# Windowed attention and a gated layer: one GpSimd select for identity and mask, and a new order of the opening table

## The chip, the core and the metric

The kernel runs on one core of a Trainium2 chip. A core has five engines with a queue of instructions each: TensorE (PE, matrix products; PEld is its loading of weights), VectorE (DVE), ScalarE (ACT), GpSimd (POOL) and SyncE (SP). Each works through its own queue in order and waits on semaphores for the others. Data moves between memory (HBM), the on-chip SBUF and the accumulators (PSUM, eight banks of 128 x 512 floats) by 16 DMA engines; loads are issued here by POOL, stores and transposes by SP. The metric is the device time of one execution in microseconds (us), as the median of several runs. Beside it stands one execution that was profiled; its span is the time from its first to its last instruction.

## The reference

Eight sequences of 576 positions, eight heads of 64. Each position attends to itself and the 63 before it; the result of all heads, 512 wide, is one token of a gated layer with 1536 hidden units.

```python
scores = (q @ k.T) / 8                      # per batch and head, 576 x 576
mask   = (rel >= 0) & (rel < 64)            # rel = query position - key position
attn   = softmax(where(mask, scores, -1e9)) # per row
x      = (attn @ v), heads side by side     # 4608 tokens x 512
g      = x @ w_gate                         # 512 -> 1536
out    = (g * sigmoid(g) * (x @ w_val)) @ w_out   # 1536 -> 512
```

## The kernel before

**Tiling.** The 4608 tokens are 36 *chunks* n of 128 and 9 *groups* c of 512 (four chunks each). Work on a chunk goes through these methods, each of which records operations on engines:

- `load_qk(n)`, `load_v(n)`: POOL issues the loads of q, k and v, with a cast to bf16 (two and one; twice as many where a chunk crosses two sequences). Buffers are rings: 6 for q and k (`NQ`), 10 for v (`NV`).
- `T`, `TE`: PE transposes q or k into a PSUM bank; ACT or DVE copies that to `qT`, `kT`. From chunk 8 on `TD` does it instead: SP issues two DMA transposes, k then q. Chunks 0 and 1 come over SP's and ACT's own queues (`first_loads`), as float, are cast by `first_cast`, transposed by `first_T` and copied by `first_ev`.
- `S(n)`: PE makes the scores in two banks, ACT takes the exponentials (line 790) into `pt`; for chunks 0 to 3 the mask is added before by a product with the identity (`bias`, line 759), for the others `M(n)` lets DVE multiply by a 0/1 mask (line 795).
- `A0`, `A1`: PE multiplies with v in two halves; a column of ones beside v (written once per buffer by `init_va`) gives the sum. `R(n, half)`: DVE's reciprocal and product (lines 875 and 878).
- `X`, `XE`: PE transposes the result, ACT or DVE copies it to `xT`. `XD` does it by a DMA transpose.

Work on a group:

- `FM(c, f, t0, t1)`: PE makes gate and value of hidden block f (of 12) for tokens t0 to t1 (line 977); `Ft`: ACT's tanh (line 996); `Fu`: DVE's two products into `uu` and `hT` (lines 1005 and 1007).
- `OM(c, u)`: twelve products with `Wo` (line 1017) make 128 rows of output; `OE`: ACT or DVE copies them, SP stores them.

Weights come in pieces by `load_w` and `load_wo`, on POOL's queue among the loads.

**Order.** The recorded operations are played on each engine in the order of recording. `_Graph.plan` finds the waits: an operation waits for the last one that wrote what it reads, or that read or wrote what it writes, unless an earlier wait of its engine covers it. Between two operations of the same engine it waits only where the second reads what the first wrote (not on PE).

The opening is a table written out by hand, `OPENING`: some 300 entries of a method, its arguments and the PSUM banks it is given. It covers the attention of chunks 0 to 11, all gated blocks of groups 0 and 1, the outputs of group 0, the scores of chunk 12 and all loads up to chunk 17. After it, `build` runs groups 2 to 8 in loops: `F` blocks, the outputs of the group before, and between them `block(n)` for the attention of chunks 12 to 19, then `pair(n)` for two chunks at a time from 20 on. `block(19)` makes chunk 20's scores on its way. At one place in group 3, the loop makes one chunk's scores alone before the pairs begin.

**What sets up the opening.** `init` (line 606) lets DVE fill the zero operand `wz` of the warm-up products, zero `ident` and `nmask`, and write the ones into all ten v buffers. POOL then makes the identity by one select over 128 x 128 (`init_pool_a`, line 625) and the additive mask by four selects over 64 x 64 (`init_mask`, line 633), and DVE the 0/1 mask from it. POOL's loads come after these five selects.

The head of the old table:

```python
    ("first_cast", ("q", 1, "act"), ()),
    ("load_qk", (2,), ()),
    ("load_v", (0,), ()),
    ("warm", (11,), (0,)),
    ("bias", (0,), (5, 3)),
```

Of the kernel before, what the change touches and what calls it, by code (L numbers as in the profile page):

```python
# [5 lines left out]
ALU = mybir.AluOpType  # L6

B, H, S, D = 8, 8, 576, 64
DM, DFF = H * D, 1536
T = B * S  # L10
# [20 lines left out]
class _Graph:  # L31
# [30 lines left out]
    def plan(self):  # L62
# [6 lines left out]
        for o in self.ops:  # L69
# [78 lines left out]
class _Program:  # L148
# [46 lines left out]
OPENING = [  # L195
    ("first_cast", ("q", 1, "act"), ()),
    ("load_qk", (2,), ()),
    ("load_v", (0,), ()),
    ("warm", (11,), (0,)),
    ("bias", (0,), (5, 3)),  # L200
    ("first_cast", ("k", None, "dve"), ()),
    ("first_T", ("k",), (6,)),
    ("first_cast", ("q", 0, "dve"), ()),
    ("first_T", ("q",), (1,)),
    ("first_ev", ("q", 0, "act"), ()),
    ("bias", (1,), (2, 4)),
    ("first_ev", ("k", 1, "dve"), ()),
    ("first_ev", ("q", 1, "act"), ()),
    ("T", ("q", 2), (7,)),
    ("load_v", (1,), ()),  # L210
    ("load_qk", (3,), ()),
    ("first_ev", ("k", 0, "dve"), ()),
    ("S", (0,), ()),
    ("T", ("k", 2), (0,)),
    ("TE", ("k", 2, "dve"), ()),
    ("load_v", (2,), ()),
    ("load_v", (3,), ()),
    ("S", (1,), ()),
    ("load_w", ("v", 0, 1), ()),
    ("bias", (2,), (1, 6)),  # L220
    ("A0", (0,), (3, 0)),
    ("load_w", ("g", 0, 1), ()),
    ("TE", ("q", 2, "dve"), ()),
    ("S", (2,), ()),
    ("load_w", ("g", 2, 4), ()),
    ("A1", (0,), ()),
    ("R", (0, 0), ()),
    ("A0", (1,), (4, 5)),
    ("A1", (1,), ()),
    ("R", (1, 1), ()),  # L230
    ("load_w", ("v", 2, 4), ()),
    ("T", ("q", 3), (7,)),
    ("T", ("k", 3), (1,)),
    ("warm", (2,), (6,)),
    ("TE", ("q", 3, "dve"), ()),
    ("bias", (3,), (5, 6)),
    ("load_qk", (4,), ()),
    ("load_w", ("v", 1, 2), ()),
    ("TE", ("k", 3, "act"), ()),
    ("S", (3,), ()),  # L240
    ("R", (1, 0), ()),
    ("A0", (2,), (7, 3)),
    ("A1", (2,), ()),
    ("R", (0, 1), ()),
    ("R", (2, 0), ()),
    ("X", (1,), (0,)),
    ("XE", (1, "act"), ()),
    ("A0", (3,), (2, 1)),
    ("R", (2, 1), ()),
    ("load_w", ("g", 1, 2), ()),  # L250
    ("A1", (3,), ()),
    ("X", (0,), (3,)),
    ("X", (2,), (5,)),
    ("XE", (2, "act"), ()),
    ("FM", (0, 0, 128, 256, 2), (4, 6)),
    ("load_w", ("g", 4, 6), ()),
    ("load_w", ("v", 4, 6), ()),
    ("R", (3, 1), ()),
    ("R", (3, 0), ()),
    ("X", (3,), (0,)),  # L260
    ("XE", (3, "act"), ()),
    ("XE", (0, "dve"), ()),
    ("FM", (0, 0, 0, 128, 2), (1, 7)),
    ("Ft", (0, 0, 0), ()),
    ("load_qk", (5,), ()),
    ("FM", (0, 0, 256, 512, 2), (3, 2)),
    ("load_v", (4,), ()),
    ("FM", (0, 2, 0, 256, 2), (0, 5)),
    ("Fu", (0, 0, 0), ()),
    ("Ft", (0, 0, 256), ()),  # L270
    ("Ft", (0, 0, 128), ()),
    ("Ft", (0, 2, 0), ()),
    ("FM", (0, 3, 0, 256, 2), (1, 7)),
    ("Fu", (0, 0, 128), ()),
    ("Ft", (0, 3, 0), ()),
    ("Fu", (0, 0, 256), ()),
    ("FM", (0, 3, 256, 512, 2), (4, 2)),
    ("T", ("q", 4), (6,)),
    ("load_qk", (6,), ()),
    ("Fu", (0, 3, 0), ()),  # L280
    ("Ft", (0, 3, 256), ()),
    ("FM", (0, 2, 256, 512, 2), (1, 3)),
    ("Fu", (0, 3, 256), ()),
    ("Ft", (0, 2, 256), ()),
    ("Fu", (0, 2, 0), ()),
    ("TE", ("q", 4, "act"), ()),
    ("FM", (0, 1, 128, 256, 2), (2, 7)),
    ("Ft", (0, 1, 128), ()),
    ("Fu", (0, 2, 256), ()),
    ("load_w", ("g", 6, 8), ()),  # L290
    ("FM", (0, 1, 0, 128, 2), (4, 0)),
    ("Ft", (0, 1, 0), ()),
# [1024 lines left out]
```

## Time and profile before

| what | value |
|---|---|
| median of 3 runs | 335.31 us (334.59 to 336.04) |
| profiled execution: time | 333.98 us |
| profiled execution: span | 331.4 us |
| granted TensorE clock, mean | 1.00 |
| PE busy | 323.7 us, 98% of the span |
| DVE busy | 224.7 us, 68% |
| ACT busy | 128.3 us, 39% |
| POOL busy | 110.7 us, 33% |
| POOL's loads (q0 software_dynamic) | 117312 packets, 18.36 MB |

The profiled execution is 2.6 us longer than its span, and 1.3 us below the median. A busy time says how long an engine worked, not what it was waited for: PE's matrix products overlap each other, and their ends are modelled, so for PE the distance from one start to the next says more than the sum of durations. A row of a timeline gives the start, the time it took, engine, source line, operation, what it writes and reads, and in brackets how long the engine sat idle before and what ended that. A row on DMA issues gives how many were issued, their size, and the median time from issue to landing.

### The profile page before, as it was taken

How to read it: one execution, taken by the hardware profiler on the slowest of the kernel's cores; microseconds unless marked ns; L12 is line 12 of the kernel's file. 1: busy time of each engine (PE TensorE's matmuls, PEld its weight loads, DVE VectorE, ACT ScalarE, POOL GpSimd, SP SyncE). 2: the span in 40 equal slices, each digit the busy share in tenths (PEclk: the TensorE clock that was granted, in tenths of full speed). 3: DMA queues.
4: the chain of work that ended last, by engine and by line, in shares of the span. 5: the costliest groups of instructions: out<-in, count | busy, mean ns of one | idle time of the engine just before them, and what ended most of it. 6: DMA issues, size and time to landing. Idle time of an engine off the chain costs nothing.

```text
span 331.4 us, 8401 instructions
## 1 busy us (share of the span) xinstructions
PE 323.7 (98%) x3511; PEld 166.2 (50%) x3511; DVE 224.7 (68%) x490; ACT 128.3 (39%) x239; POOL 110.7 (33%) x141
## 2 busy tenths in 40 slices
PE   7799899999999999999999999999999999999996
PEld 3587475555444544445454545454545444444444
DVE  5578896967866866667777777767676776565520
ACT  2756644343333543434242433333424222232222
POOL 7999993194364453333435151000000000000000
PEclk9999999999999999999999999999999999999999
DMA  9999999999999999999999999715140202000012
GB/s 169 150 177 169 171 191 141 171 135 170 169 167 148 191 154 174 173 160 158 149 126 108 135 124 130 128 53 110 47 113 33 65 33 64 34 32 35 35 60 102
DMA packets 169515, 40.19 MB, mean 121 GB/s; under 512 B 155904, under 2 KB 164992, under 8 KB 169472
## 3 DMA queue, kind: packets, MB, share of 16 engines
q0 software_dynamic: 117312, 18.36, 82.8%
q1 hardware_dynamic: 50976, 20.66, 33.3%
q10 hardware_dynamic: 1184, 0.59, 0.7%
q8 instruction: 28, 0.46, 0.6%
q14 instruction: 15, 0.12, 0.1%
HBM read 37.75 MB, written 9.44 MB: 142 GB/s over the span
## 4 chain that ended last, share of the span: by engine, by line
PE 92%; DVE 2%; POOL 2%; DMA 1%; ACT 1%; issue 1%; POOLq 0%
PE ps L977 56%; PE ps L1017 27%; PE ps L780 3%; PE ps L832 2%; PE ps L905 2%; DMA kn<-in_k_dram 1%; PE ps L1049 1%; PE ps L947 1%; DVE uu L1005 1%; POOL va L710 1%; POOL qn L647 1%; DVE hT L1007 0%; PE ps L730 0%; ACT sig L996 0%; ACT qT L664 0%
## 5 line engine op out<-in xcount | busy, mean ns | idle before, releaser
L1005 DVE SCALAR_TENSOR_TENSOR uu<-sig,ps 128x512 bf16<-128x512 bf16 (+2 forms) x122 | 76.0, 623 | 57.5 <-ACT sig L996 57.5
L977 PE MATMUL ps<-xT,Wg 128*128 128x512 bf16 (+2 forms) x488 | 113.7, 355 | 0.3
L977 PE MATMUL ps<-xT,Wv 128*128 128x512 bf16 (+2 forms) x488 | 113.3, 355 | 0.0
L996 ACT ACTIVATE sig<-ps 128x512 bf16<-128x512 f32 (+2 forms) x122 | 66.7, 551 | 82.7 <-PE ps L977 82.4
L1017 PE MATMUL ps<-Wo,hT 128*128 128x512 bf16 x420 | 95.9, 379 | 0.0
L1007 DVE SCALAR_TENSOR_TENSOR hT<-uu,ps 128x512 bf16<-128x512 bf16 (+2 forms) x122 | 76.3, 626 | 4.2
L977 PEld LDWEIGHTS ps<-xT,Wv 128*128 128x128 bf16 x488 | 47.1, 98 | 46.5 <-DVE uu L1005 0.2
L977 PEld LDWEIGHTS ps<-xT,Wg 128*128 128x128 bf16 x488 | 44.6, 98 | 42.2 <-issue 0.4
L1017 PEld LDWEIGHTS ps<-Wo,hT 128*128 128x128 bf16 x420 | 40.9, 98 | 49.2
L647 POOL DMA_DIRECT2D qn<-in_q_dram x38 | 34.9, 932 | 68.2 <-DMA qT<-qn 60.8
L790 ACT ACTIVATE pt<-ps 128x512 bf16<-128x512 f32 x72 | 38.0, 600 | 41.3 <-PE ps L780 41.2
L710 POOL DMA_DIRECT2D va<-in_v_dram x40 | 35.4, 911 | 24.0 <-PE ps L905 19.4
L664 ACT ACTIVATE ost<-ps 128x512 f32<-128x512 f32 (+2 forms) x26 | 15.0, 577 | 64.1 <-PE ps L1017 63.1
L647 POOL DMA_DIRECT2D kn<-in_k_dram x38 | 34.9, 936 | 0.9 <-issue 0.7
L795 DVE TENSOR_TENSOR pt<-pt,mask 128x512 bf16<-128x512 bf16 x64 | 23.8, 419 | 1.2 <-ACT pt L790 1.0
L666 DVE COPY ost<-ps 128x512 f32<-128x512 f32 (+1 forms) x12 | 7.9, 657 | 23.7 <-PE ps L1017 11.9
L878 DVE TENSOR_TENSOR xb<-ps,rc 128x256 bf16<-128x256 f32 x40 | 17.0, 425 | 1.4
L780 PE MATMUL ps<-qT,kT 64*64 64x64 bf16 (+1 forms) x864 | 16.0, 203 | 0.7 <-DVE kT L666 0.3
L780 PEld LDWEIGHTS ps<-qT,kT 64*64 64x64 bf16 x864 | 12.5, 108 | 6.2 <-issue 3.0
L832 PE MATMUL ps<-va,pt 64*64 64x65 bf16 x600 | 12.4, 196 | 1.5 <-issue 1.0
L832 PEld LDWEIGHTS ps<-va,pt 64*64 64x64 bf16 x600 | 8.3, 106 | 8.7 <-issue 3.0
L875 DVE RECIPROCAL rc<-ps 128x4 f32<-128x4 f32 x40 | 7.0, 175 | 6.1 <-PE ps L832 6.1
(57 smaller groups left out, 103.1 us busy)
## 6 DMA issues: line engine op xcount, KB each, us to landing
out_dram<-ost SPq DMA_DIRECT2D x35, 256.0 KB, 3.1
va<-in_v_dram POOLq DMA_DIRECT2D x32, 128.0 KB, 16.8
qn<-in_q_dram POOLq DMA_DIRECT2D x30, 128.0 KB, 15.2
kn<-in_k_dram POOLq DMA_DIRECT2D x30, 128.0 KB, 15.4
Wo<-in_moe_w_out_dram POOLq DMA_DIRECT2D x2, 768.0 KB, 16.2
Wg<-in_moe_w_gate_dram POOLq DMA_DIRECT2D x5, 256.0 KB, 6.7
Wv<-in_moe_w_val_dram POOLq DMA_DIRECT2D x5, 256.0 KB, 7.3
fk<-in_k_dram SPq DMA_DIRECT2D x1, 512.0 KB, 4.9
```

What stands on the lines that cost most here:

```text
L647: self.g.op("pool", lambda e, d=d, a=a: e.dma_start(d, a), writes=ks, dma=True)
L710: g.op("pool", lambda e, d=d, a=a: e.dma_start(d, a), writes=ks, dma=True)
L780: r = e.matmul(sv[h][o:o + 64, c, q0:q1], self.kT[ps, c, kk:kk + 64], qT[ps, c, q0:q1], start=not biased, stop=not biased or c == 3 and kk ...
L790: g.op("act", lambda e, po=po, si=si: e.activation(po, si, ACTF.Exp, scale=SCALE), reads=[bk], writes=[pk])
L795: "dve", lambda e: e.tensor_tensor(po, po, m, ALU.mult), reads=[pk, "mask"], writes=[pk]))
L832: r = e.matmul(av[half][ws, j, :], pt[ks, h, ws], vv[ks, h, 0:65], start=key == q[0], stop=key == q[-1])
L878: g.op("dve", lambda e, xo=xo, rb=rb, a=av[half]: e.tensor_tensor(xo, a[:, :, 0:64], rb, ALU.mult), reads=[bk, ("rc", ir)], writes=[("xb", ...
L977: r = e.matmul(bank[:, 0:n], W[:, kk, f * 128:f * 128 + 128], xT[:, kk, t0:t1], start=(kk == 0), stop=(kk == NK - 1))
L996: self.g.op("act", lambda e: e.activation(sig[:, 0:n], G[:, 0:n], ACTF.Tanh, scale=0.5), reads=[gk], writes=[("sig", i)])
L1005: g.op("dve", lambda e: e.scalar_tensor_tensor(uu[:, 0:n], sig[:, 0:n], 1.0, G[:, 0:n], ALU.add, ALU.mult), reads=[("sig", i), gk], writes ...
L1007: g.op("dve", lambda e: e.scalar_tensor_tensor(hT[:, f, t0:t1], uu[:, 0:n], 0.5, V[:, 0:n], ALU.mult, ALU.mult), reads=[("uu", i), vk], wr ...
L1017: r = e.matmul(OB[:, :], hT[:, f, 128 * u:128 * u + 128], self.Wo[:, f, :], start=(f == 0), stop=(f == NF - 1))
```

## The change

Four things change.

1. **The selects.** DVE fills a tile `tri` of 128 x 130 with ones, and POOL makes one select over 128 x 129 of it: one where the column is beyond the row, zero elsewhere. DVE takes the difference of two shifted views as the identity, and makes the additive mask by four multiplications of 64 x 64 of it. The 0/1 mask comes later, as an entry of the table (`mask01`), and so do the ones in the v buffers.
2. **The table.** It has the same work in another order, with other banks. Chunk 3's q and k are loaded before chunk 2's. Four half blocks of the gated layer (`FM` of blocks 3, 0, 2 and 0) stand before X(2) and X(3); in the old table X(0), X(1) and X(2) stand before the first. The loads of chunks 11, v8, 10, v10 follow `load_wo(0, 6)`, then chunk 9; in the old table it was chunk 10, 8, `load_wo(0, 6)`, 9, 11, v8. SP's transposes come in the order of chunks 8, 10, 9, 11; before it was 10, 8, 9, 11. There are 13 warm-up products in place of 14. Some copies change their engine: q0 and q1 of the first chunks, X(1), X(4), q5 and q6 go to DVE; k0, k1, X(0), q2, k7, X(10) and two output copies go to ACT.
3. **Waits.** An operation of ACT or DVE that writes what one of the last two of its own engine read or wrote now waits for that one too.
4. **The scores made alone** in group 3 are chunk 21's; in the kernel before they are chunk 20's, which `block(19)` makes too, and chunk 21's are not made there: the first pair reads for it what chunk 17 left in that buffer. The number of instructions is the same.

```diff
             for d, kind in deps:
-                if kind != "sync" and d.eng == e and not d.dma and (e == "pe" or kind != "raw") and not o.dma and e != "pool":
+                near = e != "pe" and not d.dma and npos[e] + 1 - d.pos < 3
+                if kind != "sync" and d.eng == e and not d.dma and (e == "pe" or kind != "raw" and not near) and not o.dma and e != "pool":
                     continue
...
 OPENING = [
+    ("init_va", (8, 9), ()),
+    ("warm", (11,), (7,)),
+    ("tri_select", (), ()),
+    ("ident_sub", (), ()),
+    ("warm", (1,), (6,)),
     ("first_cast", ("q", 1, "act"), ()),
+    ("load_qk", (3,), ()),
     ("load_qk", (2,), ()),
+    ("mask_half", (0,), ()),
+    ("mask_half", (64,), ()),
+    ("bias", (0,), (7, 0)),
...
     ("first_T", ("q",), (1,)),
-    ("first_ev", ("q", 0, "act"), ()),
+    ("first_ev", ("q", 0, "dve"), ()),
+    ("init_va", (0, 1), ()),
...
+    ("TE", ("q", 3, "dve"), ()),
...
+    ("mask01", (), ()),
+    ("first_ev", ("q", 1, "dve"), ()),
+    ("S", (1,), ()),
+    ("A0", (0,), (5, 0)),
+    ("A1", (0,), ()),
+    ("R", (0, 1), ()),
+    ("init_va", (1, 2), ()),
...
+    ("S", (2,), ()),
+    ("TE", ("k", 3, "act"), ()),
+    ("A1", (1,), ()),
...
+    ("S", (3,), ()),
...
+    ("load_wo", (0, 6), ()),
...
+    ("load_qk", (11,), ()),
...
+    ("load_v", (8,), ()),
...
+    ("TD", (8,), ()),
...
+    ("load_qk", (10,), ()),
...
+    ("load_v", (10,), ()),
...
+    ("load_qk", (9,), ()),
...
+    ("TD", (10,), ()),
...
+    ("TD", (9,), ()),
...
+    ("TD", (11,), ()),
...
+    ("OM", (0, 2), (3,)),
...
+    ("A0", (8,), (1, 0)),
+    ("S", (9,), (2, 4)),
...
-        g.op("dve", lambda e: e.memset(ident[:, :], 0.0), writes=["ident"])
-        g.op("dve", lambda e: e.memset(self.nmask[:, :], 0.0), writes=["nmask"])
+        g.op("dve", lambda e: e.memset(self.tri[:, :], 1.0), writes=["tri"])
...
-        self.init_va(0, self.NV)
...
+    def tri_select(self):
+        tri = self.tri[:, 0:129]
         self.g.op("pool", lambda e: e.affine_select(
-            out=ident[:, :], in_=ident[:, :], compare_op=ALU.not_equal, fill=1.0, base=0,
-            pattern=[[-1, 128]], channel_multiplier=1), writes=["ident"])
-    def init_mask(self):
-        for p0, c0, op in ((0, 0, ALU.is_ge), (0, 64, ALU.is_gt), (64, 0, ALU.is_gt), (64, 64, ALU.is_ge)):
...
+            out=tri, in_=tri, compare_op=ALU.is_ge, fill=0.0, base=-1,
+            pattern=[[1, 129]], channel_multiplier=-1), writes=["tri"])
+    def ident_sub(self):
+        self.g.op("dve", lambda e: e.tensor_tensor(self.ident[:, :], self.tri[:, 1:129], self.tri[:, 0:128], ALU.subtract),
+                  reads=["tri"], writes=["ident"])
+    def mask_half(self, p):
+        t = self.tri[p:p + 64, 1 + p:65 + p]
+        own, past = self.nmask[p:p + 64, p:p + 64], self.nmask[p:p + 64, 64 - p:128 - p]
+        self.g.op("dve", lambda e: e.tensor_scalar(own, t, 30000.0, -30000.0, ALU.mult, ALU.add),
+                  reads=["tri"], writes=[("nmask", p, 0)])
+        self.g.op("dve", lambda e: e.tensor_scalar(past, t, -30000.0, None, ALU.mult),
+                  reads=["tri"], writes=[("nmask", p, 1)])
...
         self.first_loads()
         self.init()
-        self.init_pool_a()
-        self.init_mask()
...
                     if (c, u, s) == alone:
-                        self.S(pair_from)
-                        self.M(pair_from)
+                        self.S(pair_from + 1)
+                        self.M(pair_from + 1)
                         self.share()
```

More of the change, by code (lines that the diff above doesn't have):

```diff
@@ L236 @@
[L236 to L239, printed above, removed]
+    ("X", (0,), (5,)),
+    ("warm", (1,), (4,)),
     ("S", (3,), ()),
     ("R", (1, 0), ()),
-    ("A0", (2,), (7, 3)),
-    ("A1", (2,), ()),
-    ("R", (0, 1), ()),
-    ("R", (2, 0), ()),
[L246 to L252, printed above, removed]
@@ L507 @@
-    ("OE", (0, 1, "dve"), ()),
 ]
@@ L759, in bias @@
             self.g.op("pe", lambda e, bv=bv: e.matmul(bv, self.ident[:, :], nm, start=True, stop=False),
-                      reads=["nmask", "ident"], writes=[bk])
+                      reads=[("nmask", p, i) for p in (0, 64) for i in range(2)] + ["ident"], writes=[bk])
         self.held["bias", n] = bb
```

480 lines of the change are left out of this document (240 added, 240 removed), and 11 rows, old and new, of the table OPENING.

## The prediction

> **What bounds the kernel now.** I read the page's DMA slices and chain first, then the busy time by stretch, then TensorE's timeline where it is not full.
>
> ```profile
> DMA  9999999999999999999999999715140202000012
> PE 92%; DVE 2%; POOL 2%; DMA 1%; ACT 1%; issue 1%; POOLq 0%
> ```
>
> TensorE is 92% of the chain that ends last. The DMA engines are full for the first two thirds, so a load's place in POOL's queue is a time.
>
> ```profile
> 0.00:5.70 5.70, 4.50 (x11) 1.64 (x12) 2.31 (x17) 1.49 (x2) 3.72 (x12) 1.00 0.66 182
> 5.70:19.40 13.70, 11.01 (x292) 7.14 (x290) 8.75 (x24) 8.29 (x16) 13.70 (x19) 1.00 1.96 153
> 19.40:42.40 23.00, 21.82 (x377) 15.89 (x377) 19.44 (x53) 13.90 (x32) 23.00 (x29) 1.00 1.99 174
> 42.40:83.70 41.30, 41.30 (x484) 24.07 (x473) 32.12 (x78) 16.88 (x35) 22.69 (x28) 1.00 1.80 160
> ```
>
> The columns are the stretch in us, its length, then PE, PEld, DVE, ACT and POOL. The opening table's matmuls end at 83.7. PE idles 2.7 us between 5.7 and 19.4 (13.70 - 11.01), 1.2 us up to 42.4, and not at all from there to 83.7. An order of the opening can win only what lies before 42.4, and keeps it only if loads and transposes are ready earlier too.
>
> ```profile
> 8.81 0.45 PE L780 MATMUL ps<-qT,kT 64*64 64x128 bf16 x24
> 9.52 0.45 PE L780 MATMUL ps<-qT,kT 64*64 64x128 bf16 x24
> 13.81 0.41 PE L780 MATMUL ps<-qT,kT 64*64 64x128 bf16 x22
> 15.35 0.56 PE L832 MATMUL ps<-va,pt 64*64 64x65 bf16 x17 [0.97 <-issue]
> 17.67 0.39 PE L977 MATMUL ps<-xT,Wg 128*128 128x128 bf16 x4
> 26.39 0.45 PE L780 MATMUL ps<-qT,kT 64*64 64x128 bf16 x24 [0.22 <-DVE uu L1005]
> 35.81 0.40 PE L730 MATMUL ps<-ident,kn 128*128 128x128 bf16 x4 [0.34 <-DVE uu L1005]
> 37.20 0.45 PE L780 MATMUL ps<-qT,kT 64*64 64x128 bf16 x24 [0.34 <-DVE kT L666]
> 64.96 2.75 PE L1017 MATMUL ps<-Wo,hT 128*128 128x512 bf16 x12
> 67.64 0.45 PE L780 MATMUL ps<-qT,kT 64*64 64x128 bf16 x24
> 68.02 2.76 PE L1017 MATMUL ps<-Wo,hT 128*128 128x512 bf16 x12
> 70.85 0.65 PE L780 MATMUL ps<-qT,kT 64*64 64x128 bf16 x44
> ```
>
> These are, in order: scores of chunks 0, 1 and 3; a stop of 0.97 us that no wait explains; the first matmul of the gated layer; three of the later waits; an output of group 0, the scores of chunk 9, another output, and the scores of chunk 11 (with chunk 10's).
>
> **The change, part by part.** *One select.* POOL's five selects become one.
>
> ```profile
> 1.46 0.29 POOL L625 TENSOR_SCALAR_AFFINE_SELECT ident<-ident 128x128 bf16<-128x128 bf16 x1 [1.01 <-DVE wup L612]
> 1.71 1.36 POOL L633 TENSOR_SCALAR_AFFINE_SELECT nmask<-nmask 64x64 bf16<-64x64 bf16 x4
> 3.37 1.01 POOL L647 DMA_DIRECT2D qn<-in_q_dram  x1 [0.30 <-issue]
> 37.05 1.23 POOL L647 DMA_DIRECT2D qn<-in_q_dram  x1
> 39.65 1.24 POOL L647 DMA_DIRECT2D kn<-in_k_dram  x1
> qn<-in_q_dram POOLq DMA_DIRECT2D x2, 128.0 KB, 17.5
> kn<-in_k_dram POOLq DMA_DIRECT2D x2, 128.0 KB, 17.6
> 7.37 1.29 DVE L666 COPY kT<-ps 128x512 bf16<-128x512 bf16 x2
> 1.56 1.43 DVE L621 MEMSET va<- 128x128 bf16 x10
> 14.29 1.09 ACT L790 ACTIVATE pt<-ps 128x512 bf16<-128x512 f32 x2 [0.65 <-PE ps L780]
> ```
>
> The select ends at 1.46 + 0.29 = 1.75 instead of 1.71 + 1.36 = 3.07, so the first load leaves 1.32 us earlier, and with it the whole full queue: I carry a head start of 1.32. The subtraction and four half masks go to DVE, idle then; their first readers wait on the casts of k (after 5.7) anyway. Nothing on the path; without that idle time they would cost some five short DVE operations.
>
> *Up to the first gated layer.* Chunk 0's scores still wait for the first q transpose and a strided copy of 0.65 us (half of 1.29): 8.8, as now. On DVE the copy of q for chunk 1 now stands behind two va memsets (0.14 each, a tenth of 1.43), a copy of q3 and the 0/1 mask, so chunk 1's scores come at about 10.2 (now 9.52). Chunk 2's wait for k2's copy behind R(0,1) and a memset, about 12.6. Chunk 3's wait for k3's copy, on ACT behind chunk 2's two exponentials (1.09 from 13.1, then a copy of some 0.6): about 14.7 (now 13.81). X(1), its copy and the banks it holds then put A0(2) at 16.0, and the first gated matmul at 17.1 (now 17.67). But X(2), X(3) and k4's transpose come after three half blocks. Where both kernels have done the same work, near 26, I find them level: gain 0, between -0.5 and +1 (the unexplained 0.97 may go, since the attention is less dense there).
>
> *26 to 42.4.* Now PE loses 0.9 us in the three waits shown and about as much in smaller steps, 1.9 in all by the distances of starts. In the new order k and q of a chunk are copied a block of the gated layer before their scores. I still find waits: 0.25 for k6's copy, 0.38 for a bank held by Fu(0,10), 0.30 for XE(5). That leaves 1.2 gained at 42.4, with 0.2 from before 26.
>
> *42.4 to 57.* DVE works without a gap from 40.3 to 46.8 now.
>
> ```profile
> 40.32 0.68 DVE L1005 SCALAR_TENSOR_TENSOR uu<-sig,ps 128x512 bf16<-128x512 bf16 x1
> 47.00 0.69 DVE L1005 SCALAR_TENSOR_TENSOR uu<-sig,ps 128x512 bf16<-128x512 bf16 x1 [0.18 <-ACT sig L996]
> ```
>
> The new order adds five memsets there or before (0.7) and the copies of q5, q6 and X(4) that ACT did, and gives k7's to ACT. With FM(1,1) and FM(1,4) waiting for banks that Fu(0,6) and Fu(1,3) read, 0.4 goes back: gain 0.8. Two output copies moved to ACT cost nothing: ACT is busy 16.88 of 41.30 there.
>
> *Loads and transposes.* POOL's loads and SP's transposes move with the table.
>
> ```profile
> 55.86 1.19 SPq L748 DMA_TRANSPOSE kT<-kn  x1
> 57.10 1.39 SPq L751 DMA_TRANSPOSE qT<-qn  x1
> 60.03 1.27 SPq L751 DMA_TRANSPOSE qT<-qn  x1
> 69.67 1.27 SPq L751 DMA_TRANSPOSE qT<-qn  x1
> qT<-qn SPq DMA_TRANSPOSE x1, 7.3
> qT<-qn SPq DMA_TRANSPOSE x1, 9.1
> ```
>
> These are chunk 9's two, the last of chunk 11's and of chunk 12's; the landing times are those of the second and third row. Now chunk 9's q lands at 64.4 (57.10 + 7.3) for scores at 67.64, chunk 11's at 69.1 for 70.85: 1.7 us in hand. In the new order the loads of q11, k11, v8 and v10 stand ahead of chunk 9's. Four loads, 0.87 apart ((39.65 - 37.05) / 3) with equal time to landing, are 3.5; less the head start, 2.2 later: 66.6 and 71.3, for SP still issues chunk 11 after chunk 9. The scores of 9 would be asked for at 64.96 - 0.8 - 0.5 (chunk 8's A is now behind) + 2.68 + 0.25 = 66.6: just met. Those of 11 follow 0.38 + 0.25 + 2.7 + 0.1 later, at 70.0, and wait 1.3. Behind them in PE's queue stands all else. Bounds: no wait, if the loads keep their landing; 4 us more, if chunk 10's two transposes, now just ahead of chunk 9's, delay them at the present pace (four in 69.1 - 55.86 = 13.3, 3.3 each, less the 2.6 by which chunk 10 is loaded earlier). I take 1.3, the row nearest to it being chunk 11's own.
>
> *The rest.* Waits between near operations of ACT or DVE: most were ordered by an earlier wait; some 0.05 us beside PE. One warm-up matmul more stands ahead of the bias and two fewer later, all where PE waits for casts or copies. Making chunk 21's scores instead of chunk 20's is the same instructions; its transposes were issued blocks before. Nothing.
>
> **Sum.** 0.8 - 1.3 = -0.5: the span goes from 331.4 to 331.9, and the profiled execution from 333.98 to 334.5. The median of the runs shown, 335.31, lies 1.3 above that execution; with it I forecast 335.8.
>
> [...] q and k of chunks 0 and 1 come over two other queues, which overlap the head start.
>
> ```profile
> q10 hardware_dynamic: 332, 0.17, 56.8%
> q1 hardware_dynamic: 331, 0.17, 55.9%
> ```
>
> From 3.3 to 4.3 the two move the same number of packets. [...]
>
> **Rivals.** *The transposes keep up* (loads issued earlier land earlier, chunk 11 waits nothing). For it: 1.7 us in hand now; against it: four loads put ahead. 0.8 gained: 334.5, still no change that can be told.
>
> *The early stalls go too.* If spreading removes the 0.97 stop and the other 1.7 us of idle PE before 19.4, and the transposes keep up, 0.8 + 1.0 to 2.7 is gained: 332.7. For it: these idle times are real; against it: scores 1 to 3 come later, and chunk 12's q now lands at 69.67 + 8.3 = 78.0 for scores at 78.33, so nothing runs ahead of the DMAs by more than 0.3 and the head start.
>
> ```profile
> qT<-qn SPq DMA_TRANSPOSE x1, 8.3
> 78.33 0.41 PE L780 MATMUL ps<-qT,kT 64*64 64x128 bf16 x21
> ```
>
> [...]
>
> *The transposes fall behind* (the other side). Chunk 10's transposes delay 9's and 11's; it decides from the point where chunk 11's q lands after 72.5 (70.0 + 0.8 + 1.7). For it: 3.3 us each while the queue is full; against: chunk 10 is loaded 2.6 earlier. With 3 us of wait, 2.2 lost on balance and as much again at chunk 13: 338 or so.
>
> **How the numbers follow.** The forecast 0.35, transposes keep up 0.20, early stalls go too 0.20, transposes fall behind 0.25. What a measurement of this kernel can tell from no change is about 0.5%, 1.7 us. Faster 0.20, same 0.55, slower 0.25. The range runs from 333.0 (inside the third case) to 338.0 (inside the last); the likeliest case's own is 334.3 to 336.8.
>
> **What would show it.** In the changed profile: POOL's first load at 2.05; chunk 1's scores near 10.2 and the first gated matmul near 17.1; FM(1,3) near 41.2; chunk 11's scores waiting for a transpose near 71. Wrong it would be if PE idles less than 1.5 us before 19.4, if chunk 11 finds its data, or if PE waits anew beyond 83.7.

## The result and the profile after

The changed kernel takes 338.84 us (median, 338.10 to 339.03), the kernel before beside it 334.95 us: a ratio of 1.011, with a 95% interval of 1.0076 to 1.0142. It is 3.9 us slower. Run once more, it came to 338.12 us, a ratio of 1.0095 (1.0074 to 1.0116). The forecast was 335.8, with a range up to 338.0.

The profiled execution took 339.03 us with a span of 336.3; before it was 331.4. The same stretches as before, in the windows of the changed kernel (columns: length, then PE, PEld, DVE, ACT and POOL busy, PE clock, DMA share, GB/s):

```profile
5.70:19.40 13.70, 10.17 (x276) 6.67 (x275) 7.83 (x26) 7.89 (x15) 13.70 (x19) 1.00 2.11 168
19.40:42.40 23.00, 19.23 (x316) 14.64 (x319) 19.22 (x59) 13.09 (x30) 23.00 (x29) 1.00 1.89 179
42.40:83.70 41.30, 38.70 (x512) 23.06 (x518) 29.83 (x72) 15.84 (x34) 21.16 (x26) 1.00 1.98 162
```

PE idles 3.5 us in the first stretch (2.7 before), 3.8 in the second (1.2) and 2.6 in the third (none). Some of that is not real, since 39 records of matmuls are missing; the weight loads (PEld) are all there, so positions and stops are read from them from here on.

The timeline of weight loads of the changed kernel has four places where TensorE stands still inside an operation:

```profile
16.62 0.14 PEld L853 LDWEIGHTS ps<-va,pt 64*64 64x64 bf16 x7 [0.69 <-DVE xT L687]
17.36 0.75 PEld L853 LDWEIGHTS ps<-va,pt 64*64 64x64 bf16 x57 [0.60 <-issue]
...
31.57 0.28 PEld L801 LDWEIGHTS ps<-qT,kT 64*64 64x64 bf16 x18
32.35 0.11 PEld L801 LDWEIGHTS ps<-qT,kT 64*64 64x64 bf16 x2 [0.51 <-issue]
...
37.46 0.10 PEld L998 LDWEIGHTS ps<-xT,Wg 128*128 128x128 bf16 x1
40.27 0.53 PEld L998 LDWEIGHTS ps<-xT,Wg 128*128 128x128 bf16 x3 [2.71 <-issue]
...
80.69 0.34 PEld L801 LDWEIGHTS ps<-qT,kT 64*64 64x64 bf16 x23
82.75 0.10 PEld L801 LDWEIGHTS ps<-qT,kT 64*64 64x64 bf16 x1 [1.72 <-issue]
```

The last pair shows best what this is. Chunk 12's scores are 24 matmuls of one operation, and an operation waits in front of its first instruction only. Yet 23 of them run and the 24th comes 2.06 us after the first. No wait of the program can stand there. The counts of weight loads up to the four places:

```profile
0.00:17.30 17.30, 12.58 (x219) 6.92 (x220) 8.34 (x31) 8.90 (x16) 16.08 (x25) 1.00 1.62 172
0.00:32.30 32.30, 26.90 (x467) 18.72 (x469) 20.55 (x71) 16.98 (x36) 31.08 (x44) 1.00 1.80 172
0.00:40.20 40.20, 31.92 (x591) 22.05 (x594) 27.70 (x93) 21.87 (x46) 38.98 (x53) 1.00 1.82 174
0.00:82.70 82.70, 71.75 (x1091) 45.52 (x1100) 58.11 (x164) 37.61 (x79) 62.34 (x80) 1.00 1.89 169
```

220, 469, 594 and 1100 weight loads: the distances are 249, 125 and 506, which is 2, 1 and 4 times about 125. The kernel before stopped at the same kind of place: its 0.97 us of the prediction stands behind weight load 221, and this row behind 597 (counted in the same way):

```profile
37.57 0.33 PEld L977 LDWEIGHTS ps<-xT,Wg 128*128 128x128 bf16 x3
38.27 0.10 PEld L977 LDWEIGHTS ps<-xT,Wg 128*128 128x128 bf16 x1 [0.36 <-issue]
```

The page of the changed kernel has a queue of instruction packets, beside the queue of GpSimd's loads:

```profile
q0 software_dynamic: 117312, 18.36, 80.5%
q8 instruction: 28, 0.46, 0.5%
```

28 packets of 16 KB (0.46 MB in 28), on average one for each 125 of the 3510 pairs of weight load and matmul: by this count they carry TensorE's instructions, a block each. In the traces of the two kernels every stop named here ends 1.4 to 1.7 us after the end of such a packet. The packet that ends the longest stop is seen in the DMA view of 37.5 to 39.5 us, as the one slice (of 0.05 us) with 479 GB/s, at 37.9:

```profile
GB/s 197 205 146 169 184 182 182 479 184 172 164 143 151 141 166 159 154 148 164 151 151 131 151 148 167 148 159 144 164 156 141 154 151 156 161 159 169 164 166 146
...
q8 instruction: 1, 0.02, 2.9%
```

From 160 to 310 us, where a slice of the page has at most 136 GB/s (up to 193 earlier), the packet for the next block starts within some 2 us of the moment at which TensorE begins the block ahead of it, in both kernels: the one at 175.5 us in the changed kernel, for example, 1.1 us after weight load 2101, at 174.4. By these times, in these two executions, only one block is fetched ahead, when its predecessor begins. TensorE stood still where it had used up a block of 125 pairs before the next was there, and chunks' scores and attention use it up fast: A0, S and A1 are 56 pairs in 0.64 us, a block of the gated layer 8 pairs in 1.7 us. In the opening of the changed kernel the packets came some 2 to 6.3 us after the beginning of the block ahead, and another 2.4 us go by (0.94 of packet, 1.5 to the first instruction). At the longest stop, the block behind weight load 469 was used up in 5.2 us (32.35 to 37.56), its successor's packet started after 5.55, and TensorE went on at 40.27.

### The profile page after: what moved, and what is told of

It reads as the page before. It is cut to its first block, busy times and chain, and to the rows that moved or that the text cites. A ratio compares the mean times of both kernels' runs of the same rounds, so it can differ in the third digit from the quotient of the medians.

```text
span 336.3 us, 8352 instructions
## 1 busy us (share of the span) xinstructions
PE 319.2 (95%) x3471; PEld 166.0 (49%) x3510; DVE 223.6 (66%) x492; ACT 128.9 (38%) x241; POOL 110.0 (33%) x137
## 3 DMA queue, kind: packets, MB, share of 16 engines
q0 software_dynamic: 117312, 18.36, 80.5%
q1 hardware_dynamic: 50976, 20.66, 32.9%
## 4 chain that ended last, share of the span: by engine, by line
PE 87%; DVE 5%; issue 2%; ACT 2%; DMA 2%; POOL 1%
PE ps L998 52%; PE ps L1038 26%; PE ps L801 3%; PE ps L853 2%; DVE uu L1026 2%; DMA va<-in_v_dram 2%; PE ps L926 2%; DVE hT L1028 1%; ACT sig L1017 1%; PE ps L1070 1%; DVE xb L899 1%; ACT pt L811 1%; PE ps L968 1%; POOL qn L668 1%; POOL kn L668 1%
## 5 line engine op out<-in xcount | busy, mean ns | idle before, releaser
L998 PE MATMUL ps<-xT,Wg 128*128 128x512 bf16 (+2 forms) x465 | 108.7, 354 | 6.2 <-DVE xb L899 2.9
L998 PEld LDWEIGHTS ps<-xT,Wg 128*128 128x128 bf16 x488 | 44.8, 98 | 46.0 <-issue 2.9
L731 POOL DMA_DIRECT2D va<-in_v_dram x40 | 36.4, 943 | 22.8 <-PE ps L926 22.8
L685 ACT ACTIVATE ost<-ps 128x512 f32<-128x512 f32 (+2 forms) x28 | 16.2, 578 | 65.8 <-PE ps L1038 62.0
L668 POOL DMA_DIRECT2D kn<-in_k_dram x38 | 35.1, 931 | 0.0
L687 DVE COPY ost<-ps 128x512 f32<-128x512 f32 (+1 forms) x10 | 6.5, 651 | 23.2 <-PE ps L1070 11.8
L801 PE MATMUL ps<-qT,kT 64*64 64x64 bf16 (+1 forms) x864 | 16.5, 203 | 3.5 <-issue 2.0
```

The lines of the kernel that those rows point to most:

```text
L668: self.g.op("pool", lambda e, d=d, a=a: e.dma_start(d, a), writes=ks, dma=True)
L731: g.op("pool", lambda e, d=d, a=a: e.dma_start(d, a), writes=ks, dma=True)
L801: r = e.matmul(sv[h][o:o + 64, c, q0:q1], self.kT[ps, c, kk:kk + 64], qT[ps, c, q0:q1], start=not biased, stop=not biased or c == 3 and kk ...
L998: r = e.matmul(bank[:, 0:n], W[:, kk, f * 128:f * 128 + 128], xT[:, kk, t0:t1], start=(kk == 0), stop=(kk == NK - 1))
```

## The experiments

Three theories stood at the start. Theory I: these stops are late instruction blocks. Theory W: they are waits of single operations, as the waits of the changed kernel from 36 to 42 us have it (what was waited for, us in total, times, longest):

```profile
PE ps L998 <- DVE xb L899: 2.9, 1, 2.9
```

Theory H: the early loads are what hurts. Later, B and C are two accounts of why a block comes late: loads queued ahead of it, or accidents of timing. The short names of the kernels are those of the texts. Times are medians; the kernel before took 334.8 to 335.2 us beside them.

### The order and the loads, one at a time

*old_table*: the changed kernel with the order of before in the table (the edit is shown against the kernel before).

```diff
 OPENING = [
+    ("init_va", (0, 10), ()),
+    ("tri_select", (), ()),
+    ("ident_sub", (), ()),
+    ("mask_half", (0,), ()),
+    ("mask_half", (64,), ()),
+    ("mask01", (), ()),
...
```

> The order of the opening table goes back to that of before; the select, the half masks, the waits between near operations and chunk 21's scores stay as changed. Theory I (TensorE's own instructions arrive late: its stream comes in blocks of about 125 weight loads, the next block is asked for when the one before it begins, and TensorE stands still where it has used a block up before the next is there): the blocks again end where they did before (about weight loads 221, 347, 472, 597), with few matmuls wasted, so the stops are again about 1 us near weight load 220 and under 0.7 us near 597, and the time is 334.0 to 336.0 us. Theory W (the stops are waits of single operations for VectorE in the new order) gives the same here. Theory H (the loads that leave 1.3 us earlier are what hurts, through the packets they take from fq and from later fetches): the earlier loads are still there, so the time stays above 337 us.

*late_loads*: the changed kernel with its loads held back.

```diff
+        for p0, c0 in ((0, 0), (0, 64), (64, 0), (64, 64)):
+            d = self.spare[p0:p0 + 64, c0:c0 + 64]
+            self.g.op("pool", lambda e, d=d: e.affine_select(
+                out=d, in_=d, compare_op=ALU.is_ge, fill=0.0, base=0,
+                pattern=[[1, 64]], channel_multiplier=-1), writes=["spare"])
...
```

> The changed kernel with four more 64x64 selects on an unused tile behind the one select, so that GpSimd's loads leave about 1.3 us later, as they did before. Theory I (late instructions): the stops stay at weight loads 220, 469, 594 and 1100 with other lengths, the front gives back about 0.3 us (fq lands earlier); time 337.5 to 340 us. Theory H (the head start of the loads is what hurts): time 334.5 to 336.5 us.

*old_late*: both edits.

> The order of the opening table of before, the select and the rest as changed, and the loads held back by four extra selects: with the three kernels there are (order before or changed, loads early or late) this is the fourth cell. If the early loads are the cause, whatever the order, the stop near weight load 221 is again about 1 us (2.3 us with the loads early) and the time 334.2 to 335.4 us. If the select, the half masks or the waits between near operations cost something of their own: 335.5 to 336.5 us.

| | loads early | loads 1.15 us later |
|---|---|---|
| order of before | old_table 335.98, ratio 1.0040 (1.0021 to 1.0058) | old_late 334.72, 0.9984 (0.9956 to 1.0012) |
| changed order | changed kernel 338.84, 1.0109 (1.0076 to 1.0142) | late_loads 334.78, 1.0000 (0.9983 to 1.0017) |

This settles what of the change costs the time. The select, the half masks, the near waits and chunk 21 cost nothing that can be told (old_late). Nor does the new order (late_loads), and neither order gains anything. Loads that leave early cost some 1.3 us in the old order and 4 in the new one. The granted clock is not the reason in the new order: in executions with a mean clock of 1.00, the changed kernel took 337.59 to 339.03 us (five runs, with those of *again* below), late_loads 333.83 to 336.18 (all twelve). Nor are the extra selects themselves: flight9 below has none and came to 335.28. For late_loads theory H had the right number and theory I the wrong one (337.5 to 340); for old_table it was the other way round, with H above 337. Both hold a part: the early loads are the cause, and they act through the late blocks. One size was missed in both kernels with the old order: the stop behind weight load 221 was to be about 1 us, and PE's rows have 2.3 us of idle in old_table and 1.6 in old_late (0.97 before). In late_loads the weight loads have the same numbers and the same order, and the timeline of PE has these rows at the two longest stops (lines stand 7 further down):

```profile
36.42 0.32 PE L860 MATMUL ps<-va,pt 64*64 64x65 bf16 x16
37.50 1.02 PE L1005 MATMUL ps<-xT,Wg 128*128 128x512 bf16 x4 [0.76 <-DVE uu L1033]
...
77.95 0.63 PE L808 MATMUL ps<-qT,kT 64*64 64x128 bf16 x24
```

The step between the two weight loads behind number 594 is 0.83 us in place of 2.80, and chunk 12's 24 matmuls stand in one row, with 0.21 us ahead of the last weight load in place of 1.83. The block that begins behind weight load 469 (at 31.5) has its packet at 35.1, in the twelfth slice of the DMA view of 34.5 to 36.5:

```profile
GB/s 205 184 195 195 215 184 205 215 195 172 184 522 179 174 184 166 156 151 144 166 177 151 154 146 174 169 144 148 161 184 146 154 146 159 159 149 164 151 169 169
...
q8 instruction: 1, 0.02, 2.9%
```

That is 3.6 us after the block begins, against 5.55 (32.35 to 37.9) in the changed kernel. By the starts of the same operations, the changed kernel is 0.25 us behind late_loads at the first gated matmul (behind the stop at 220), 0.52 more at the stop behind 469, 2.0 more at 594 and 1.6 more at 1100: 4.4 us, and none anywhere else up to there. Behind that late_loads loses 0.8 again, at a wait of chunk 13's scores for their transpose, so the spans differ by 3.7.

In old_table the first stop is the long one, behind weight load 221 (13.99 to 16.55 in PE's timeline), and it costs twice: the granted clock is at half speed for some 3 us behind it. Eleven of the twelve runs of old_table have a mean clock of 0.995 or 0.99, against four of twelve in old_late; so a part of the 1.3 us in the old order is clock.

```profile
13.99 0.29 PE L844 MATMUL ps<-va,pt 64*64 64x65 bf16 x13
16.55 0.56 PE L844 MATMUL ps<-va,pt 64*64 64x65 bf16 x17 [2.28 <-issue]
...
18.00:20.00 2.00, 1.74 (x28) 1.61 (x21) 1.73 (x6) 0.59 (x2) 2.00 (x4) 0.50 1.99 178
20.00:22.00 2.00, 2.00 (x21) 1.84 (x20) 0.39 (x2) 0.86 (x3) 2.00 (x4) 0.68 1.46 190
```

### A place in the stream or an operation

*swap10*: FM(0,10) goes ahead of chunk 5's attention, with its two banks exchanged.

```diff
+    ("Fu", (0, 2, 256), ()),
+    ("FM", (0, 10, 0, 512, 2), (6, 0)),
     ("A0", (5,), (5, 2)),
-    ("Fu", (0, 2, 256), ()),
     ("S", (7,), (3, 1)),
     ("TD", (10,), ()),
     ("A1", (5,), ()),
-    ("FM", (0, 10, 0, 512, 2), (0, 6)),
```

> The changed kernel with one gated block, FM(0,10), moved ahead of chunk 5's attention and chunk 7's scores (Fu(0,2,256) ahead of it). The block behind the longest stop runs 56 weight loads earlier. Theory I (late instructions): the stop stays at weight load 594 of TensorE's stream, which is now inside A1(5), and is shorter by the 1.7 us of gated matmuls that now lie ahead of it: about 1.1 us instead of 2.8; the stops near 220 and 1100 stay; time 336.5 to 338.0 us. Theory W (FM(0,10) waits for VectorE's second piece of xb for chunk 5, as the profile's row names it): FM(0,10) no longer waits, nothing stops inside A1(5), and the 2.8 us go or reappear in front of the block behind A1(5).

PE's timeline of swap10:

```profile
38.62 0.26 PE L853 MATMUL ps<-va,pt 64*64 64x65 bf16 x8
39.85 0.26 PE L853 MATMUL ps<-va,pt 64*64 64x65 bf16 x8 [0.97 <-issue]
40.03 1.04 PE L998 MATMUL ps<-xT,Wg 128*128 128x512 bf16 x4
```

The stop now cuts A1(5) in half, behind weight load 593 of the stream (594 expected), and is 1.2 us long between weight loads (1.1 expected). The block that had stopped runs through. Theory W is out: the row that named DVE's xb only named the event that came last before TensorE went on. The stops near 220 and 1100 were expected to stay; the one at 220 shrank to 0.37 us of idle, and at 1100 only a step of 0.22 was left. The time was 337.95 us (1.0070 to 1.0120).

*pad94*: the place of everything in the stream is moved by 88 weight loads.

```diff
-    ("warm", (11,), (7,)),
+    ("warm", (5,), (7,)),
+    ("tiny", (94,), (7,)),
...
+    def tiny(self, count):
+        bank, bk = self.bank("f")
...
+                r = e.matmul(bank[0:64, 0:64], self.wz[0:64, 0:64], self.wz[0:64, 0:64], start=True, stop=True)
...
```

> The changed kernel with 6 of the 11 long warm-up matmuls at the start replaced by 94 very small ones, in time in which TensorE waits for the first loads. No operation of the rest is moved; each stands 88 weight loads later in the stream. Theory I (late instructions): the stops stay at the same numbers of weight loads and so move to other operations: none at FM(0,10) and none at S(12); possible ones near weight load 348 (end of A1(2), 1 to 3 us), 596 (in S(6), under 1 us), 975 to 1101 (S(9), S(10), under 1.5 us). In sum 1 to 4 us less than now: 335.0 to 338.0 us. Theory W (waits of operations): FM(0,10) still stops for 2.8 us and S(12) for 1.8 us, time 338.3 to 339.5 us.

PE's timeline and windows of pad94:

```profile
18.09 0.77 PE L864 MATMUL ps<-va,pt 64*64 64x65 bf16 x46 [0.52 <-DVE xT L688]
20.72 0.34 PE L864 MATMUL ps<-va,pt 64*64 64x65 bf16 x18 [1.86 <-issue]
...
41.08 0.32 PE L864 MATMUL ps<-va,pt 64*64 64x65 bf16 x16
41.33 1.04 PE L1009 MATMUL ps<-xT,Wg 128*128 128x512 bf16 x4
...
20.70:22.70 2.00, 1.91 (x30) 1.34 (x30) 1.62 (x7) 0.38 (x1) 2.00 (x4) 0.81 2.06 168
22.70:24.70 2.00, 2.00 (x15) 1.57 (x13) 1.32 (x6) 0.66 (x2) 2.00 (x3) 0.50 1.82 180
```

There is no stop at FM(0,10) nor in S(12); there is one behind weight load 348, in A1(2), as expected. The expected time (335.0 to 338.0) was missed: 338.81 us (1.0095 to 1.0145). The stop at 348 was followed by half speed of TensorE's clock for some 3.5 us, which no expectation had; FM(0,2) for 256 tokens takes 1.70 us there (23.15 to 24.85), 0.88 in the changed kernel (19.78 to 20.66). By the starts, the first attention came 1.5 us later as well; its row names the load of v.

### How early, and how many loads at a time

*late_one*, *late_half*, *late2*: one, two and eight extra selects in place of the four of late_loads. *flight11*, *flight10*, *flight9*, *flight6*, *flight4*: the loads leave early, but fewer are under way.

```diff
-    LANES = {"pool": 16, "sp": 16, "act": 8}
+    LANES = {"pool": 9, "sp": 16, "act": 8}
```

*late_flight9*: that cap of 9 and the four selects. *hold20*: the four selects stand ahead of the 20th load. *again*: the changed kernel.

> The changed kernel with eight extra 64x64 selects on an unused tile behind the one select: GpSimd's loads leave some 2.4 us later than in the changed kernel, twice the delay that brought the time back to that of before. Theory B (TensorE's instruction blocks wait behind the loads that are queued when the block is asked for, so less head start means shorter waits): the waits for a block stay short, 2 to 4 us from the block's beginning to its packet, no stop above 1 us behind weight load 345; but the front now waits for data, so 334.5 to 336.5 us. Theory C (each wait for a block is an accident of timing, and any shift of the loads draws new ones): some waits are again 5.5 us or more and the time lies anywhere from 334 to 339 us.

> The changed kernel with two extra selects, the loads some 0.6 us later than there. Theory B (waits for instruction blocks grow with the loads queued ahead): between the changed kernel and the one with four extra selects, 335.0 to 338.0 us. Theory C (accidents of timing): anywhere from 334 to 339 us, not between.

> The changed kernel with one extra select, the loads 0.25 to 0.3 us later than there; with two (0.55 us) the time was that of before. Theory B (the waits for instruction blocks are set by the loads queued when the block is asked for): more is queued at 23 us than with the cap of 10, where the waits were 5.9 and 5.5 us, so the waits behind weight loads 344 and 469 are again 5.5 to 6.3 us and the time 337.5 to 339 us. Theory F (it is the first loads leaving at the very beginning that sets the order of things for the blocks, and any hold there cures it): waits of 2.5 to 4 us, time 334.5 to 336 us.

> The changed kernel, loads leaving early as there, but at most 6 of GpSimd's loads are under way at a time (16 before): each load waits until the sixth before it has landed. Theory B (instruction blocks wait behind queued loads): with less queued, the block behind weight load 469 and those behind 594 and 1100 come 1 to 3 us sooner, the stops shrink to under 1 us each, and the time is 334.5 to 336.5 us. Theory C (accidents of timing): the time lies anywhere from 334 to 339.5 us, with one or more waits for a block of 5.5 us or more.

> The same with at most 4 of GpSimd's loads under way. Theory B: waits for a block shorter still, 2 to 4 us, no stop above 0.7 us behind weight load 345; against it the fifth and later loads leave some 2 us later than in the changed kernel, which chunk 0's and 1's attention feels by up to 1 us: 334.0 to 337.0 us. Theory C: waits for a block of 5.5 us or more remain, 334 to 340 us.

> The changed kernel with at most 9 of GpSimd's loads under way. With 6 the waits for blocks were short but loads came too late. Theory B: loads of the first 24 us are untouched, the wait for the block behind weight load 345 stays near 6 us, that behind 469 shrinks from 5.5 to 4 to 5 us, so the stop at 594 is 1 to 2 us instead of 2.8; time 336 to 338.5 us.

> The loads held back by four extra selects and at most 9 of them under way. If both shorten the waits for blocks without delaying data that is waited for, the stop of 0.8 us at weight load 594 goes and the time is 333.5 to 334.7 us; if the held-back loads then come too late for chunks 5 to 8, 335 to 337 us.

> The changed kernel itself once more, beside the two caps on one chip. Theory B (instruction blocks wait behind queued loads): the waits behind weight loads 344 and 469 are again near 6.2 and 5.5 us, the stop at 594 near 2.8 us, time 338 to 339.3 us. Theory C (accidents of timing): other waits, time anywhere from 334 to 339 us.

> The changed kernel with at most 10 of GpSimd's loads under way: the cap first binds at the 20th load, which leaves 0.5 us later; the first 19 leave as in the changed kernel. Theory B: that half microsecond less of queued loads is what the delay by two selects also took, and there the waits behind weight loads 344 and 469 fell to 3.4 and 3.5 us; the same here, the stop at 594 under 1.2 us, time 334.5 to 336.5 us. Theory C: no such tie.

> The changed kernel with at most 11 of GpSimd's loads under way: by the landing times of the changed kernel the cap does not bind before some 34 us, so up to there the loads are the same. Theory B: the waits behind weight loads 344 and 469 stay near 6.2 and 5.5 us and the stop at 594 near 2.8 us; time 337.5 to 339.3 us. Theory C: other waits, time anywhere from 334 to 339 us.

> The changed kernel with four extra selects on an unused tile directly in front of the 20th load of GpSimd (chunk 5's); the first 19 loads leave as early as in the changed kernel, those behind about 1.2 us later. Theory B: the loads queued from 23 us on are then those of the kernel with everything held back, so the waits behind weight loads 344 and 469 are 2.5 to 4 us, the stop at 594 under 1.2 us and the time 334.5 to 336.5 us. Theory F (the first loads decide): waits of 5.5 us or more, 337.5 to 339.5 us.

The table has, from each profiled execution, when GpSimd's 28th load leaves; the time from the beginning of a block (the weight load in the heading) to the start of the next block's packet; and the step between weight loads at the two later stops (0.2 without a stop at 594, 0.02 at 1100). All in us.

| kernel | median (interval of the ratio) | 28th load | behind 344 | behind 469 | step at 594 | behind 973 | step at 1100 |
|---|---|---|---|---|---|---|---|
| again | 338.12 (1.0074 to 1.0116) | 23.1 | 6.3 | 5.5 | 2.80 | 4.7 | 0.98 |
| flight11 | 339.41 (1.0118 to 1.0163) | 23.15 | 6.2 | 5.6 | 2.80 | 5.4 | 1.74 |
| changed | 338.84 (1.0076 to 1.0142) | 23.2 | 6.3 | 5.55 | 2.80 | 6.0 | 1.83 |
| late_one | 337.55 (1.0058 to 1.0126) | 23.3 | 3.6 | 3.7 | 0.93 | 5.9 | 1.74 |
| flight10 | 338.13 (1.0085 to 1.0135) | 23.7 | 5.9 | 5.5 | 2.80 | 5.6 | 1.47 |
| late_half | 335.06 (0.9969 to 1.0024) | 23.7 | 3.4 | 3.5 | 0.59 | 4.3 | none |
| late_flight9 | 336.17 (0.9981 to 1.0050) | 24.25 | 3.5 | 3.8 | 0.94 | 6.1 | 1.82 |
| flight9 | 335.28 (0.9977 to 1.0029) | 24.35 | 2.5 | 3.6 | 0.93 | 5.9 | 2.02 |
| late_loads | 334.78 (0.9983 to 1.0017) | 24.5 | 3.3 | 3.6 | 0.83 | 4.0 | 0.21 |
| hold20 | 335.60 (1.0005 to 1.0055) | 24.55 | 5.3 | 3.5 | 0.75 | 4.1 | 0.22 |
| late2 | 337.16 (1.0044 to 1.0111) | 25.7 | 3.1 | 4.0 | 1.21 | 5.8 | 2.09 |
| flight6 | 339.05 (1.0088 to 1.0189) | 29.3 | 2.7 | 2.3 | none | 4.9 | 0.53 |

The profiles are single executions. Those of late_one, late_half, flight10 and hold20 fell on the shortest of their runs, those of flight9 (337.44) and of the changed kernel on the longest. The ratio of late_flight9 leaves out two of its twelve runs, of 339.39 and 339.45 us.

The wait behind 469 makes the long stop at 594. It is 5.5 us in the three kernels at the top that hold nothing back up to 23 us, and in swap10, and at most 4.0 us in all six that send the 28th load a microsecond or more later. In between, at a delay of 0.1 to 0.5 us, it goes both ways. The work that DMA has done does not differ: by 23.5 us it had taken 16,297 packets of GpSimd's loads with the cap of 9 and 16,306 in the changed kernel, though the cap held the 28th load back by 1.15 us. So the wait does not go by DMA's progress. That speaks for theory B, the queued loads, with four reservations.

First, the queue alone does not tell all kernels apart. Flight10 missed its expectation: from the 20th load on its loads leave with those of late_half, and its waits were 5.9 and 5.5 us against 3.4 and 3.5. Flight9 and hold20 hold back the same loads, from the 20th on (18.0 and 18.2 us, 16.9 in the changed kernel), and their waits behind 344 were 2.5 and 5.3 us. (The expectation of flight9 took the loads up to 24 us for untouched, which they were not.)

Second, at late_one the same program goes both ways: its six runs took 334.98, 336.01, 336.64, 338.45, 338.87 and 339.02 us, and the profile fell on the first. So its short waits, against the 5.5 to 6.3 us expected, say nothing of the other runs. The first three have a mean granted clock of 1.00, the last three of 0.994 to 0.999. In late2, flight6 and late_flight9 the runs fall into two groups by the clock in the same way: in late2, 335.60 to 337.50 us at 1.00, and 338.45 to 340.14 below. So a part of what looks like accident goes with the clock; what lowers it in those runs is not shown, since most have no profile.

Third, the wait behind 973, and with it the stop at 1100, does not follow the head start: some 6 us in late_one, late2 and both caps of 9, 4 to 4.3 in late_half, late_loads and hold20, 4.2 in swap10. This stop, 1.6 us of the loss in the changed kernel's profile, is an accident of timing in the sense of theory C, as far as these runs show.

Fourth, old_table and pad94 hold nothing back either, and behind the blocks nearest to 469 (472 and 473) their packets came after 3.9 us, behind 347 and 348 after 2.8 and 5.2. Early loads alone do not make a wait long; it also matters when the block is asked for.

Theory F (the first loads decide) does not fit the time of hold20, whose first 19 loads leave as early as in the changed kernel. By what path inside DMA a queued load delays an instruction packet, and why just there, stays open.

The packets of these loads are short: GpSimd's 117,312 took 80.5% of 16 engines in 336.3 us, 0.037 us each. By that the waits of 5.5 and 6.3 us are the time of some 150 and 170 of them on one engine, an estimate from the page's figures.

Holding back has its own price. late2 missed 334.5 to 336.5: its profile is 2.4 us later at the first gated matmul's second product (21.2 against 18.8 us) and so loses what it gains; in that execution the clock was also at half from 11.6 to 18.4 us (mean 0.990). flight6 missed the same range: it has shorter waits and no stop for a block but those at 220 and, of half a us, in chunk 12's scores, yet it is 1.3 us behind the changed kernel at k5's transpose (27.35 against 26.04) and, past 594, loses some 2 us more up to chunk 9's scores: data that come late. late_flight9 still has its stop at 594 (0.94), which was to go. flight4 took 349.15 us (1.0395 to 1.0477), where 334 to 340 was expected; 6.5 us are lost by k5's transpose (32.50).

### Can the loss be mended on TensorE's side

*late_swap*: late_loads with the edit of swap10. *half_om*: late_half with an output block ahead of chunk 12's scores.

```diff
+    ("OM", (0, 1), (0,)),
     ("S", (12,), (5, 2)),
     ("XE", (11, "act"), ()),
     ("A1", (10,), ()),
-    ("OM", (0, 1), (0,)),
```

> The changed kernel with the loads held back by four extra selects and with FM(0,10) ahead of chunk 5's attention. With the loads held back a stop of 0.8 us was left at weight load 594. Theory I (late instruction blocks): 1.7 us of gated matmuls more lie in front of that weight load, so the stop there goes and the time is 333.5 to 334.8 us (held back alone: 334.8). If each order draws its own accidents, 334.5 to 337 us.

> The kernel with two extra selects (loads 0.6 us later, 335.1 us), with the output block OM(0,1) moved ahead of chunk 12's scores, so that 12 more long matmuls lie in front of weight load 1100, where a stop of 1.8 to 2.0 us stood in some kernels. Theory I (late instruction blocks): a block that comes 6 us after it is asked for no longer stops TensorE there; in executions that had the stop 1.5 to 2 us are gained, against 0.3 us of waiting for a bank in all: median 334.0 to 335.2 us, with a smaller spread.

PE's timelines of the two, late_swap first:

```profile
40.31 0.81 PE L1005 MATMUL ps<-xT,Wg 128*128 128x512 bf16 x3 [1.27 <-ACT pt L818]
```

```profile
82.52 0.40 PE L975 MATMUL ps<-ident,xb 128*128 128x128 bf16 x4 [1.32 <-DVE xb L906]
```

Both did away with their stop: none at 594 in late_swap, none at 1100 in half_om, though the block behind 973 there took 6.3 us. And both lost more to a wait that the moved block had covered: FM(0,6) needs a bank that the exponentials of chunk 7 still read, and X(10) now stands right behind A1(10), whose results DVE has yet to scale. They took 336.99 us (1.0022 to 1.0088) and 335.77 (1.0008 to 1.0040), both above what theory I expected. No kernel of the study is measurably faster than the one before.

## Why the prediction was wrong

It forecast 335.8 us, no change; the kernel is 3.9 us slower and 0.8 outside the range. Point by point:

*One select.* The work on DVE did cost nothing (old_late). The first load left at 1.67 us, not 2.05:

```profile
1.43 0.30 POOL L640 TENSOR_SCALAR_AFFINE_SELECT tri<-tri 128x129 bf16<-128x129 bf16 x1 [0.91 <-DVE wup L628]
1.67 1.01 POOL L668 DMA_DIRECT2D qn<-in_q_dram  x1
```

A head start of 1.70 in place of 1.32. **The step that failed is its sign.** "I carry a head start of 1.32" went into the sum only as data that come earlier. It costs 4 us in the new order. No rival had this: all four cases took early loads to be good or harmless. Of the sum 0.8 - 1.3, neither term was found: the order gained nothing that can be told, and chunk 11 waited for nothing.

*The 0.97 stop.* "A stop of 0.97 us that no wait explains" was left open, as something that may go if the attention is less dense. This was the one row that pointed to the cause: it is an instruction block that comes late (its packet lies at 13.0 to 13.9 us, and TensorE goes on at 15.35), and it was used as a possible gain, not as a stop that could grow elsewhere.

*The start of the table.* Scores of chunks 0 to 3 came at 9.2, 10.3, 13.2 and 15.3 us (forecast 8.8, 10.2, 12.6, 14.7), the first gated matmul at 18.2 (17.1); with the loads held back at 17.9. The mechanism (copies in line) fits the row of chunk 3, whose first weight load waits 0.48 us for ACT's copy of k; the sizes are 0.1 to 1.1 short, and a part of the last is the stop at 220.

*26 to 57 us.* FM(1,3) came at 44.8, forecast 41.2; 42.1 with loads held back, of which 0.6 is the rest of the stop at 594. The order's own gain of 0.8 is not found: late_loads equals the kernel before within 0.2%.

*Chunk 11's scores* were to wait 1.3 us for their transpose. They do not wait, nor do chunk 9's:

```profile
70.24 0.32 PE L853 MATMUL ps<-va,pt 64*64 64x65 bf16 x16
70.39 0.42 PE L801 MATMUL ps<-qT,kT 64*64 64x128 bf16 x24
...
73.63 0.32 PE L853 MATMUL ps<-va,pt 64*64 64x65 bf16 x12
73.79 0.41 PE L801 MATMUL ps<-qT,kT 64*64 64x128 bf16 x21
...
60.01 1.60 SPq L772 DMA_TRANSPOSE qT<-qn  x1
```

Chunk 11's last transpose is issued at 60.0 and landed 6.3 us later, at 66.3, not at 71.3. The four loads put ahead did not push chunk 9's back by 2.2 us: its q and k landed at 53.9 and 54.7, ahead of the 54.9 and 55.8 of before. The rival "the transposes keep up" was right in this and wrong in its gain.

*The two other queues.* fq, the load of q for chunks 0 and 1, took 5.7 us before and 6.1 in the changed kernel, but 6.4 with the loads held back, so the 0.4 us more are not borne out as the head start's. These are the rows of the changed kernel and of late_loads:

```profile
fq<-in_q_dram ACTq DMA_DIRECT2D x1, 512.0 KB, 6.1
```

```profile
fq<-in_q_dram ACTq DMA_DIRECT2D x1, 512.0 KB, 6.4
```

*The transposes fall behind.* That the time lies near the 338 of this case is chance: no scores up to chunk 11 waited for a transpose that was issued by DMA. Its sum does not come out either: 2.2 us and as much again, from 335.3, are 339.7.

*What would show it wrong* named less than 1.5 us of idle before 19.4, chunk 11 finding its data, and waits beyond 83.7. Only the second came true; what did the damage stood in none of them.

## What to carry to other kernels

When TensorE stops inside an operation and the row says "issue", count its weight loads up to there. Here the stops at multiples of about 125 (behind weight loads 220, 469, 594 and 1100 of the changed kernel) were late instruction blocks, and the releaser that a row named for the matmul behind one meant nothing. Short matmuls by the dozen (scores, attention, transposes) use up a block in a few us (5.2 behind weight load 469), so what fills DMA's queues just then, even loads that come in good time, can be paid for by TensorE, here with some 4 us. A transfer that leaves earlier is no gain in itself; price it by who asks for it, and look at what shares the queues.

## What was not expected

A stop of about 2 us in the opening was followed by half of TensorE's clock in old_table (0.50 from 17.9 to 21.3 us) and pad94 (0.50 from 21.9 to 25.3). The stop of 2.8 us at 594 was not, in the changed kernel (1.00 from 40.2 on), though in flight11 the block behind it ran at half speed (0.50 from 39.8 to 43.2, a mean of 0.995). Each of these three stretches of half speed is 3.4 us long, and late2's from 11.6 to 18.4 is twice that. How long PE had stood still does not tell the cases apart: it was busy for 0.28 of 2.5 us in old_table (14.0 to 16.5), for 0.16 of 2.0 in pad94 (18.7 to 20.7), and for 0.04 of 2.7 in the changed kernel (37.5 to 40.2), where the clock stayed at 1.00. What sets off the half speed does not come out of these runs.
